# Duo attention and an MLP on one core: the program's order written anew, a zero fill in two copies

## The chip, the cores and the metric

The kernel runs on one core of one Trainium2 chip. Its time is the device time of one execution in microseconds, the median of several runs. A profiled execution gives the trace, whose span runs from the first to the last instruction.

## The reference, cut

```python
# q, k, v: 4 batches x 8 heads x 768 positions x 64, float32
keep[retrieval heads 0, 2, 6] = causal
keep[other heads]             = causal & (key is one of the first 4 | query - key < 64)
a = softmax(where(keep, q @ k.T / 8, -1e9));  x = (a @ v) as 3072 tokens x 512
h = x @ w_in                                  # 512 -> 2048
g = maximum(h, 0) + alpha * minimum(h, 0)     # alpha: one slope for each of the 2048
out = g @ w_out                               # 2048 -> 512, float32
```

## The kernel before

The 32 heads are 16 pairs, numbered n = 0 to 15, four to a batch: in a pair one head stands on partitions 0 to 63 and the other on 64 to 127. The 3072 tokens are eight pieces of the MLP, t = 0 to 7, two to a batch (512 and 256 tokens). Batch 0's attention comes first; from then on the MLP of one batch lies between the attention of the next, so that TensorE has work all along.

Nothing in the program is scheduled by a planner. Each step is an *item* with a name, and `ORDER` is a string of some 1240 names kept in the program. Python walks through it once, and each engine runs what it is given in just that order. The item, not the engine, decides where an instruction runs. So an engine whose next instruction waits for data holds up all that stands behind it on this engine.

The names that matter here (n is the pair, h the head in it, m a part, t the piece of tokens, f a block of the 2048):

- `L` loads of q, k, v on SyncE's DMA queue (SP); `Cq`, `Ck`, `Cv` casts to bf16, by GpSimd (POOL), ScalarE (ACT) or VectorE (DVE) for the first pairs, as the lists CQ, CK, CV say. `Cv` on GpSimd has copies of the sink rows with it (line 342).
- `Tq`, `Tk` transposes of q and k on TensorE (lines 404, 406), `tq`, `tk` the copies from PSUM into `qT` and `kT` (411; 429, 435 to 437). From pair 8 on `Dq`, `Dk` are DMA transposes on SP's queue instead.
- `kz0` to `kz3`, `qz`, `qz0`: zero fills of the parts of `kT` and `qT` that no copy writes, one `kz` for each of the first pairs. `kz2` alone is a copy of a zero by ScalarE.
- `S` scores (TensorE, lines 456, 473, 505, 544), `s` their exponentials on ScalarE (512, 560, 566), `m` masks on VectorE (522, 571).
- `A` the product with v (TensorE, 595), `r`, `a` the division by the sums on VectorE (607, 614) into `xn`.
- `X`, `x` the transposition of `xn` into `xT`: on TensorE for pairs 0 to 3 and 15 (628), by a DMA transpose on SP's queue for pairs 4 to 14 (622).
- `P` the first product of the MLP (648), `p` the relu of -h on ScalarE (653), `g` the slopes on VectorE (660). `P0.f` is cut into three items, `P2`, `P4`, `P6` into two, and the first of the two needs only the first three of the batch's four head pairs that `PAIRS` orders; `xT` of a batch comes from four `X`.
- `O0.s.u` the second product of piece 0 (668), quarter u of the 2048; `o0.s` copies and stores it by GpSimd's queue (678). For the pieces from 1 on the second product is made of seven block products: `Z`, `Q`, `b`, `D` (711, 726, 744, 692).
- `wi..` and `wo0` to `wo3` the loads of the weights, in six and four DMAs on GpSimd's queue (827, 832, 836). Quarter u of `O0.s.u` reads what `wo`u loads.
- `warm0` to `warm8`: matmuls of zeros into a bank that nobody reads (822), of 32, 3, 14, 4, 4, 4, 4, 4 and 4 instructions. They keep TensorE busy.

```python
    for name in ORDER:
        if not beside_burst(name):
            emit_burst()
        I[name]()
```

`emit_burst` gives the saved 64-row score matmuls of both heads of a pair to TensorE in turn. PSUM has eight banks, which items take and give in the order of `ORDER`.

Of the kernel before, what the change touches and what calls it, by code (L numbers as in the profile page):

```python
# [19 lines left out]
S2.0.2 X0 s2.0.1 x0 wi6 Tq3 S2.0.0 warm6 tk3.1 s2.0.2 A1.0 tq3 wi7 r1.0 s2.0.0 A1.1 S2.1.0 wi5 S3.0.0 r1.1 a1.0 Lv3 A2.0  # L20
Cv3.0 Lq4 a1.1 wi4 X1 x1 s2.1.0 s3.0.0 S3.0.1 r2.0 S2.1.1 Cv3.1 s3.0.1 P0.3.0 s2.1.1 S3.1.0 A2.1 a2.0 Lk4 Cq4 S3.1.1
s3.1.0 r2.1 Ck4.0 a2.1 s3.1.1 P0.0.0 A3.0 A3.1 r3.0 a3.0 P0.1.0 r3.1 Tq4 X2 a3.1 P0.2.0 X3 Lq5 Lk6 x2 Lq6 P0.3.1 wi2 x3
Lk5 P0.1.1 wi3 tq4 Ck4.1 P0.2.1 near1 P1.0 P0.2.2 P0.1.2 p0.2 P0.0.1 P0.0.2 Tk4 p0.1 tk4.0 P0.3.2 p1.0 g0.1 p0.0 ro1
g1.0 P0.14 Cq5 near0 P1.14 tk4.1 g0.0 wo1 P0.15 p1.14 P0.13 p0.15 Tq5 g0.15 Lq7 P1.2 p0.13 P0.8 wo0 Lk7 g0.2 g1.14 p0.3
wo3 p0.8 nr g0.3 P0.9 Cq6 p0.9 P0.11 P0.10 g0.8 g0.9 P1.8 tq5 Ck5.1 Ck5.0 g0.13 p0.11 P1.10 p0.14 wo2 P0.4.0 Tq6 g0.11
P0.5.0 P0.5.1 Lv5 g0.14 p1.8 g1.8 p1.2 kfz1 P1.6 p0.10 Lv6 P0.4.1 P0.5.2 g1.2 p1.10 P0.4.2 tq6 g1.10 p1.6 g0.10 Tk5 P0.6
g1.6 near2 ns tk5.0 P0.12 p0.6 g0.6 p0.5 S4.1.0 p0.4 P0.7 s4.1.0 p0.12 P1.12 Ck6.1 S5.0.0 g0.4 Ck6.0 O0.1.0 g0.12 tk5.1
p1.12 Tk6 g0.5 g1.12 p0.7 D1.0 O0.0.0 P1.4 tk6.1 g0.7 tk6.0 s5.0.0 O0.0.1 S5.1.1 S5.0.2 p1.4 S6.1.1 m4.1.0 D1.1 g1.4
S5.1.0 S4.0.1 Lv4 Ck7.1 O0.1.1 O0.0.2 s6.1.1 Cq7 O0.1.2 D2.1 S4.0.0 Z1.0.1 S5.1.2 s5.0.2 S6.1.2 s5.1.0 S4.1.2 s5.1.1
S4.0.5 s4.0.1 S4.0.3 Ck7.0 s4.0.0 s5.1.2 D2.0 O0.0.3 m5.1.0 O0.1.3 Lq8 m4.0.0 m5.1.1 s4.0.3 Cv5 s4.1.2 S4.1.5 S4.1.1  # L30
m4.0.1 s4.0.5 S4.0.4 S4.0.2 s6.1.2 O0.2.0 m5.0.2 O0.2.1 m4.0.3 S6.1.0 Cv4 m5.1.2 s4.0.4 Tk7 m4.0.5 Z1.0.3 o0.0 s4.1.1
m5.0.0 m4.0.4 A5.1 r5.1 s4.1.5 Lk8 a5.1 s4.0.2 s6.1.0 Cv6 A4.0 Ck8 Lk9 tk7.1 Tq7 tk7.0 O0.2.2 r4.0 S6.0.2 S5.0.1 O0.2.3
m6.1.2 tq7 S6.0.0 o0.1 m4.1.5 Q1.0.1 a4.0 s6.0.2 m6.1.0 m6.1.1 S6.0.3 S4.1.4 S4.1.3 s6.0.0 S6.0.4 s5.0.1 S7.1.1 Cq8
O0.3.0 s6.0.3 s4.1.3 o0.2 Z1.0.2 Lv7 m5.0.1 m6.0.3 s6.0.4 A5.0 Ck9 Lq9 s4.1.4 r5.0 S6.0.5 S7.0.0 m4.1.3 s6.0.5 s7.0.0
O0.3.1 A6.1 S6.0.1 a5.0 Dk8.0 m4.1.1 S7.1.0 m6.0.4 b1.1.0 s6.0.1 m6.0.0 m4.1.4 s7.1.1 O0.3.2 Cq9 S7.0.2 m6.0.5 Dq8
S7.0.1 A4.1 r6.1 Cv7 Dk9.0 a6.1 m7.1.1 O0.3.3 m6.0.1 s7.1.0 s7.0.1 r4.1 S8.1.1 s7.0.2 m7.0.2 S7.1.2 a4.1 S8.0.0 m7.0.1
S8.0.4 m7.0.0 s7.1.2 X5 o0.3 A6.0 s8.0.0 m7.1.0 A7.0 m7.1.2 s8.1.1 Dq9 r6.0 a6.0 A7.1 r7.0 Q1.0.2 S8.1.0 Lq10 S8.0.1
S9.0.0 s8.0.4 S9.0.1 S9.1.0 kfz2 r7.1 X4 X6 a7.1 a7.0 s8.0.1 s9.1.0 X7 nz0 Q1.0.5 D4.0 S8.0.5 Lk10 s9.0.1 Z1.0.4 S9.1.2
s9.0.0 m10.0.2 S9.0.2 Q1.0.6 b4.1.0 s8.1.0 Q1.0.3 S8.0.2 D3.0 S8.1.4 s8.0.5 b2.1.0 s9.1.2 S9.1.1 b7.1.0 S8.0.3 Lk11
s9.0.2 s8.0.2 Cq10 s8.1.4 P2.11.0 D4.1 P2.8.0 P2.3.0 b3.1.0 Lv9 s8.0.3 P2.4.0 P2.12.0 m8.0.1 m8.0.0 m9.0.2 P2.4.1  # L40
P2.12.1 m4.1.2 m9.0.0 Dq10 m9.1.2 s9.1.1 D3.1 p2.4 m8.1.0 P2.3.1 P2.8.1 m9.0.1 p2.3 m8.0.4 P2.2.0 m9.1.1 Q1.0.7 m9.1.0
b8.1.0 p2.12 m8.1.1 P2.7.0 P2.2.1 g2.4 P2.11.1 P2.7.1 p2.8 g2.3 p2.2 P2.1.0 g2.12 P2.6.0 P2.0.0 Lq11 P2.0.1 P2.1.1
P2.6.1 g2.8 m8.0.5 m8.0.3 Ck11 Lv8 p2.11 g2.2 P3.4 P2.5.0 p2.6 g2.11 Cv9 b5.1.0 Ck10 P2.13.0 p2.1 g2.6 p2.0 P2.5.1
P2.13.1 g2.1 p2.7 P2.10.0 P2.10.1 p2.5 g2.7 P3.12 Lv11 g2.5 p3.4 Dk11.0 A9.1 p2.10 g2.0 Q1.0.4 P2.14.0 p2.13 g2.10 p3.12
P2.9.0 r9.1 Cq11 P2.14.1 g3.4 P2.9.1 p2.9 Cv8 g2.13 b6.1.0 P2.15.0 g2.9 P2.15.1 Q2.1.1 p2.14 g3.12 P3.0 g2.14 Q2.0.1
b1.2.1 p2.15 a9.1 Lv10 g2.15 A8.0 r8.0 Q2.1.2 Dk10.0 S8.1.5 S8.1.3 b1.2.0 p3.0 Z2.1.1 S10.0.0 S10.0.5 a8.0 Z2.1.3 s8.1.5
Q2.0.2 Dk10.1 s10.0.0 Dq11 A9.0 s8.1.3 Lq12 Q2.1.5 b7.2.1 b7.2.0 S10.1.1 g3.0 s10.0.5 S10.0.1 b4.2.1 S11.0.0 S10.0.4
S11.1.1 S11.1.0 r9.0 Z2.1.2 a9.0 s11.0.0 s10.1.1 s11.1.1 Z2.0.1 m4.0.2 Q2.1.6 s11.1.0 s10.0.4 Z2.1.4 P3.8 S11.0.2
S11.0.1 S10.1.2 b2.2.1 m8.1.3 Lk13 Z2.0.3 b3.2.1 S10.1.0 Lv14 Q2.1.7 m11.1.0 Cv10 m10.1.1 Q2.1.3 Lq13 s10.0.1 S10.0.2
# [35 lines left out]
def kernel(  # L85
# [237 lines left out]
    def item(name, fn, *args):  # L323
        I[name] = lambda: fn(*args)
# [681 lines left out]
```

## Time and profile before

| | |
|---|---|
| median of 3 runs | 221.5 us (221.34 to 221.97) |
| the profiled execution's own time | 222.12 us |
| its span | 220.4 us, so 1.7 us lie around it |
| TensorE matmuls busy | 213.7 us, 97% |
| VectorE busy | 186.6 us, 85% |
| ScalarE busy | 146.4 us, 66% |
| GpSimd busy | 46.7 us, 21% |
| moved by DMA | 35.98 MB |

The profiled execution took 0.6 us more than the median of the runs. Busy time of TensorE is counted from pipelined matmuls, so a share of 97% says that it was hardly ever without an instruction, not that each column took its shortest time. Where TensorE waited is read from the start times in the timeline, and what it waited for from the releaser in brackets at the end of a row.

### The profile page before, as it was taken

The numbers are of one execution on the slowest core, as the hardware profiler recorded it, in microseconds if no ns is written. First come the engines' busy times: TensorE is split into PE (matmuls) and PEld (weight loads), VectorE is DVE, ScalarE is ACT, GpSimd is POOL, SyncE is SP. The second block draws the span as 40 slices with busy tenths as digits, with TensorE's granted clock in tenths as the row PEclk, the third lists the DMA queues.
The fourth block names the chain that finished last, engine by engine and source line by source line (L and its number), as shares of the span: only waits on it lengthen the run. The fifth ranks groups of instructions, "written<-read, shape, count | busy, mean of one in ns | idle before, by whom it ended". The sixth has DMA issues, their size and how long they took to land.

```text
span 220.4 us, 5765 instructions
## 1 busy us (share of the span) xinstructions
PE 213.7 (97%) x2194; PEld 158.0 (72%) x2210; DVE 186.6 (85%) x471; ACT 146.4 (66%) x314; POOL 46.7 (21%) x92
## 2 busy tenths in 40 slices
PE   8999999999999999999999999999999999999993
PEld 8788976665466765568789646678888645788882
DVE  6679658999989987999999999999999669799741
ACT  4689638999999794565972375589995066563330
POOL 6659990620412200003020200010010100000000
PEclk9999999999999999999999999999999999999999
DMA  5999999999999999999998699692027110011033
GB/s 170 329 212 212 313 240 226 233 204 210 205 241 199 224 179 230 222 186 192 205 232 157 147 244 201 143 206 70 4 97 111 51 48 0 3 48 48 3 145 142
DMA packets 89655, 35.98 MB, mean 163 GB/s; under 512 B 76676, under 2 KB 87964, under 8 KB 89628
## 3 DMA queue, kind: packets, MB, share of 16 engines
q1 hardware_dynamic: 83484, 26.35, 59.7%
q0 software_dynamic: 5824, 8.93, 17.7%
q8 instruction: 17, 0.28, 0.6%
q10 hardware_dynamic: 320, 0.34, 0.5%
q14 instruction: 10, 0.08, 0.1%
HBM read 27.58 MB, written 6.29 MB: 154 GB/s over the span
## 4 chain that ended last, share of the span: by engine, by line
PE 85%; DMA 7%; SPq 2%; POOL 2%; DVE 1%; issue 1%; ACT 0%; POOLq 0%
PE P L648 38%; PE P L726 27%; PE P L595 6%; PE P L668 6%; DMA rows<-in_k_dram 4%; PE P L473 4%; DMA xT<-xn 3%; PE P L406 2%; SPq L254 1%; PE P L466 1%; POOL w_in_b L827 1%; SPq L277 1%; PE P L628 1%; PE P L456 1%; DVE eS L571 1%
## 5 line engine op out<-in xcount | busy, mean ns | idle before, releaser
L648 PE MATMUL P<-xT,w_in_b 128*128 128x256 bf16 (+1 forms) x501 | 88.2, 325 | 1.0 <-DMA xT<-xn 0.4
L660 DVE SCALAR_TENSOR_TENSOR g<-neg,oma,P 128x256 bf16<-128x256 f32 (+1 forms) x128 | 72.0, 608 | 11.1 <-ACT neg L653 10.4
L653 ACT ACTIVATE neg<-P 128x512 f32<-128x512 f32 x96 | 55.1, 601 | 30.9 <-PE P L648 23.5
L648 PEld LDWEIGHTS <-w_in_b 128*128 128x128 bf16 x512 | 49.2, 98 | 30.3 <-DMA xT<-xn 0.7
L726 PEld LDWEIGHTS <-g 128*128 128x128 bf16 x480 | 45.6, 98 | 8.2 <-issue 1.0
L726 PE MATMUL P<-w_out_b,g 128*128 128x256 bf16 x320 | 40.0, 273 | 0.0
L512 ACT ACTIVATE eR<-P 128x448 bf16<-128x448 f32 (+4 forms) x63 | 36.6, 630 | 5.1 <-PE P L473 2.6
L744 POOL DMA_DIRECT2D out_dram<-ot x14 | 7.9, 565 | 113.9 <-ACT ot L768 46.7
L560 ACT ACTIVATE eS<-P 128x352 bf16<-128x352 f32 x45 | 20.1, 488 | 1.5 <-PE P L473 1.3
L614 DVE TENSOR_TENSOR xn<-P,rcp 128x448 bf16<-128x448 f32 (+1 forms) x32 | 18.7, 598 | 0.6 <-DVE rcp L607 0.2
L668 PE MATMUL P<-w_out_b,g 128*128 128x512 bf16 x59 | 15.1, 380 | 0.3
L571 DVE TENSOR_TENSOR eS<-eS,ms_near 128x352 bf16<-128x352 bf16 x45 | 14.7, 347 | 0.0
L711 DVE TENSOR_TENSOR g<-g 128x1024 bf16<-128x1024 bf16 x20 | 13.5, 684 | 0.1
L456 PE MATMUL P<-qT,kT 128*128 128x192 bf16 (+14 forms) x68 | 11.1, 251 | 0.2 <-ACT eS L566 0.2
L473 PE MATMUL P<-qT,kT 64*128 64x176 bf16 (+8 forms) x175 | 11.3, 250 | 0.0
L595 PE MATMUL P<-vb,eS 128*128 128x65 bf16 x260 | 10.8, 193 | 0.0
L595 PEld LDWEIGHTS <-eS 128*128 128x128 bf16 x260 | 9.9, 97 | 1.2 <-issue 0.2
L522 DVE TENSOR_TENSOR eR<-eR,mr_near 128x128 bf16<-128x128 bf16 (+5 forms) x54 | 10.2, 221 | 0.2 <-ACT eR L512 0.2
L726 PE MATMUL P<-w,g 128*128 128x256 bf16 x80 | 10.2, 273 | 0.0
L595 PE MATMUL P<-vb,eR 128*128 128x65 bf16 x276 | 10.1, 193 | 0.0
L473 PEld LDWEIGHTS <-kT 64*128 64x128 bf16 x175 | 6.8, 94 | 4.4 <-issue 4.0
L607 DVE RECIPROCAL rcp<-P 128x7 f32<-128x7 f32 (+1 forms) x32 | 6.0, 194 | 4.7 <-PE P L595 3.1
(130 smaller groups left out, 269.3 us busy)
## 6 DMA issues: line engine op xcount, KB each, us to landing
out_dram<-ot POOLq DMA_DIRECT2D x18, 256.0 KB, 3.2
rows<-in_k_dram SPq DMA_DIRECT2D x21, 192.0 KB
rows<-in_q_dram SPq DMA_DIRECT2D x18, 192.0 KB
rows<-in_v_dram SPq DMA_DIRECT2D x17, 192.0 KB
rows<-in_v_dram SPq DMA_DIRECT2D x14, 196.0 KB
rows<-in_q_dram SPq DMA_DIRECT2D x7, 384.0 KB
w_out_b<-in_moe_w_out_dram POOLq DMA_DIRECT2D x4, 512.0 KB, 16.2
rows<-in_k_dram SPq DMA_DIRECT2D x9, 196.0 KB
```

The lines of the kernel that those rows point to most:

```text
L473: nc.tensor.matmul(to, keys[own], queries[own], start=True, stop=True)
L512: nc.scalar.activation(ebuf[n, hh][:, lo:hi].rearrange("p (x c) -> p x c", x=len(parts)), P[:, got[0]:got[0] + len(parts), 0:(hi - lo) // ...
L560: nc.scalar.activation(slots, sc[:, 0:352].rearrange("p (s c) -> p s c", c=176), AF.Exp, scale=scale)
L571: nc.vector.tensor_tensor(slots, slots, ms_near[:, 0:2, :] if m == 0 else ms_near[:, 1:3, :], op=ALU.mult)
L595: nc.tensor.matmul(pav[:, i, :], e[:, o:o + 128], vv[:, j, hh, 0:D + 1], start=(m == 0), stop=(m == len(terms) - 1))
L614: nc.vector.tensor_tensor(xn[n][:, 0:nt, D * hh:D * hh + D], pav[:, :, 0:D], rcp.to_broadcast([128, nt, D]), op=ALU.mult)
L648: nc.tensor.matmul(psg[:, w * i:w * (i + 1)], w_in_b[:, c, 128 * fb:128 * (fb + 1)], xT[:, c, o:o + w], start=(x == 0), stop=(x == 3))
L653: nc.scalar.activation(neg[t, f], bank(held["P", t, f][0]), AF.Relu, scale=-1.0)
L660: nc.vector.scalar_tensor_tensor(g_buf[t % 2][:, fb, 0:w], neg[t, f][:, c], oma[:, fb:fb + 1], bank(got[0])[:, c], op0=ALU.mult, op1=ALU.add)
L668: nc.tensor.matmul(bank(held["O", t, s][0]), g_buf[t % 2][:, f, 128 * s:128 * (s + 1)], w_out_b[:, f, :], start=(f == 0), stop=(f == 15))
L711: nc.vector.tensor_tensor(to, x0, x1, op=op)
L726: nc.tensor.matmul(q_bank(t, u, CHAIN[y]), left[t, u][y][:, f, :], right[y][:, f, :], start=(first and f == 0), stop=(f == 7), skip_group_ ...
```

## The change

Two things differ. The zero fill of pair 2's half of `kT` becomes two copies, one for each head, `kz2` and `kz4`, so that they can stand at two places of the order:

```diff
-    item("kz2", nc.scalar.copy, kT_all[:, 2].rearrange("p h c -> p (h c)"), zero.to_broadcast([128, 2 * 7 * 128]))
+    for hh in range(2):
+        item(f"kz{2 * hh + 2}", nc.scalar.copy, kT_all[:, 2, hh], zero.to_broadcast([128, 7 * 128]))
```

And `ORDER` is written anew: nearly all of its lines differ. All other items are the same, and each stands once. SP's queue gets its loads and transposes in the same order as before. The lines of the program behind the fill move down by one. The first lines of the table:

```diff
-busy zero id warm0 kz3 Lq0.0 sz1 vz2 nms nmr so1 vz0 Lq0.1 Lk1 warm8 warm5 warm3 kz1 qz0 one Lq1 Lk0 La Ck0.0 kz2 Cq0.0
-Tq0.0 tq0.0 Tk0.0 qz warm2 Lk2 Lq2 kz0 tk0.0 Ck1.0 Ck1.1 Cq0.1 Tk1 S0.0.1 s0.0.1 Tq0.1 S0.0.0 Cq1 warm7 Lv0 tk1.0 sz2
...
+busy zero id warm0 kz3 Lq0.0 sz1 vz2 nms nmr so1 vz0 Lq0.1 Lk1 Lq1 Lk0 La Cq0.1 Ck0.0 kz0 sz2 kz1 Cq0.0 idf qz0 Ck1.0
+warm8 Tq0.0 Ck1.1 kz4 Tk0.0 Lk2 tk0.0 warm2 tq0.0 Cq1 vo S0.0.0 kz2 Tk1 s0.0.0 S0.0.2 s0.0.2 kfz0 warm5 ro0 Ck0.1 vz1
...
```

Ahead of the first transposes TensorE had 44 matmuls of zeros (`warm0` with 32, `warm8`, `warm5` and `warm3` with 4 each); now it has 36 (`warm0`, `warm8`), and `warm5` and `warm3` come among the first scores. The sum over the program is the same.

ScalarE's first rows, from the cast of pair 0's keys on; before:

```order
L364 CAST g_85<-rows 128x6x64
L324 COPY kT<-zero 128x1792
L411 COPY qT<-P 64x768
L512 ACTIVATE eR<-P 128x896 x2
L411 COPY qT<-P 128x768
L512 ACTIVATE eR<-P 128x896
L566 ACTIVATE eS<-P 128x4x192
L512 ACTIVATE eR<-P 128x896
```

And with the change:

```order
L364 CAST g_85<-rows 128x6x64
L324 COPY kT<-zero 128x896
L411 COPY qT<-P 64x768
L324 COPY kT<-zero 128x896
L512 ACTIVATE eR<-P 128x896 x2
L411 COPY qT<-P 128x768
L512 ACTIVATE eR<-P 128x896
L566 ACTIVATE eS<-P 128x4x192 x2
L512 ACTIVATE eR<-P 128x896 x3
```

The first `L411` is `tq0.0`, the second `tq1`; the `eR` rows are pair 0's exponentials and the `eS` rows pair 1's. Half of the zero copy moved behind `tq0.0`, and the two first exponentials of pair 1 now come one behind the other.

VectorE in the same part of the program. The row `qT 128x4x16` is `qz`, the two rows of line 429 are `tk0.0`, and each three of lines 435 to 437 are the copies of pair 1's keys for one head (`tk1.0`, `tk1.1`). Before, up to `tk1.1`:

```order
L324 MEMSET qT 128x4x16
L324 MEMSET kT 128x896
L429 COPY kT<-P 64x258
L429 COPY kT<-P 64x510
L435 COPY kT<-P 64x6x124
L436 COPY kT<-P 64x20
L437 COPY kT<-P 64x7x4
L324 MEMSET eS 128x6x32
L324 MEMSET rows 128x128 x2
L435 COPY kT<-P 64x6x124
L436 COPY kT<-P 64x20
L437 COPY kT<-P 64x7x4
```

And with the change, from `tk0.0` to `qz`:

```order
L429 COPY kT<-P 64x258
L429 COPY kT<-P 64x510
L324 MEMSET vb 128x70
L324 MEMSET eR 128x164
L324 MEMSET rows 128x128
L435 COPY kT<-P 64x6x124
L436 COPY kT<-P 64x20
L437 COPY kT<-P 64x7x4
L435 COPY kT<-P 64x6x124
L436 COPY kT<-P 64x20
L437 COPY kT<-P 64x7x4
L324 MEMSET qT 128x4x16
```

`qz` stood ahead of `tk0.0`; now it stands behind both heads of `tk1`, ahead of `tq0.1`.

GpSimd among the first loads of weights; `g_85` are the casts of the first pairs' queries and keys, `vb` values. Before, from `wi1a`, `wi0a`, `wi1b`, `wi0b` (line 827) on:

```order
L827 DMA w_in_b<-in_moe_w_in_dram 64x2x512 x4
L351 CAST g_85<-rows 128x2x6x64
L391 CAST vb<-rows 128x14x64
L342 COPY vb<-vb 4x6x32 x2
L391 CAST vb<-rows 128x14x64
L342 COPY vb<-vb 4x6x32
L832 DMA w_in_b<-in_moe_w_in_dram 64x4x512 x3
```

And with the change:

```order
L827 DMA w_in_b<-in_moe_w_in_dram 64x2x512 x2
L391 CAST vb<-rows 128x14x64
L342 COPY vb<-vb 4x6x32 x2
L351 CAST g_85<-rows 128x2x6x64
L827 DMA w_in_b<-in_moe_w_in_dram 64x2x512 x2
L391 CAST vb<-rows 128x14x64
L342 COPY vb<-vb 4x6x32
L832 DMA w_in_b<-in_moe_w_in_dram 64x4x512 x2
```

Pair 1's values (`Cv1`) and pair 3's queries (`Cq3`) come between the first and the second half of the early weight loads instead of behind them. Further down the last two loads of `w_out_b` (`wo3`, `wo2`) now both stand behind the masks `nr` and `ns` (lines 794 to 812), where `wo3` stood ahead of both and `wo2` between them.

Further on: TensorE comes to the first matmul that reads `wo2` through `O0.1.2`, where it came to it through `O0.0.2`, and the scores `S4.1.0`, `S5.0.0`, `S6.1.1` that stood ahead of it stand behind it. GpSimd stores `o0.1`, `o0.2`, `o0.0`, `o0.3` in this order instead of 0, 1, 2, 3. The first product of piece 2 begins with `P2.7.0` instead of `P2.11.0`, after the same matmuls. Behind these the order within the pieces differs everywhere, with the same items.

More of the change, by code (lines that the diff above doesn't have):

```diff
@@ L20 @@
[L20 to L49, printed above, removed]
@@ L80 @@
-Q6.0.4 Z6.1.4 b3.7.0 b6.6.0 Z7.0.4 Q6.1.4 Q6.1.3 Q7.0.7 b7.6.1 b6.6.1 b8.6.1 b5.7.0 Q7.0.3 Q7.0.4 b8.7.0 b6.7.0
+busy zero id warm0 kz3 Lq0.0 sz1 vz2 nms nmr so1 vz0 Lq0.1 Lk1 Lq1 Lk0 La Cq0.1 Ck0.0 kz0 sz2 kz1 Cq0.0 idf qz0 Ck1.0
+warm8 Tq0.0 Ck1.1 kz4 Tk0.0 Lk2 tk0.0 warm2 tq0.0 Cq1 vo S0.0.0 kz2 Tk1 s0.0.0 S0.0.2 s0.0.2 kfz0 warm5 ro0 Ck0.1 vz1
+tk1.0 S0.0.1 tk1.1 qz Ck2.1 Al Tq1 Lq2 Tq0.1 Ck2.0 Lv0 Cq2 Lk3 warm4 warm3 tq0.1 tq1 Tk0.1 s0.0.1 sz0 S1.1.0 Cv0 s1.1.0
+Lv1 warm7 S1.0.0 Ck3.0 Ck3.1 tk0.1 Tk2 s1.0.0 Lq3 wi1a S0.1.0 warm6 so0 tk2.0 one wi0a s0.1.0 S0.1.1 Tq2 S0.1.2 Cv1 Cq3
@@ new lines @@
+s0.1.1 wi1b wi0b vz3 A0.0 S1.0.1 s0.1.2 al tk2.1 Lv2 A0.1 tq2 r0.0 S1.1.1 s1.0.1 r0.1 Tk3 S2.0.1 s1.1.1 a0.0 S2.0.2 a0.1
+A1.0 s2.0.1 tk3.0 r1.0 A1.1 Cv2 Lv3 a1.0 Lq4 r1.1 s2.0.2 Lk4 Tq3 S2.0.0 a1.1 Lq5 tq3 S2.1.0 X0 wi6 s2.0.0 X1 x1 s2.1.0
+wi7 Cv3.0 S3.0.0 x0 S2.1.1 A2.0 tk3.1 wi5 s3.0.0 wi4 S3.0.1 s2.1.1 so2 A2.1 Lk6 s3.0.1 Ck4.1 r2.0 Ck4.0 S3.1.0 a2.0
+P0.3.0 S3.1.1 wi2 s3.1.0 A3.0 s3.1.1 r2.1 a2.1 Cq4 Cv3.1 r3.0 P0.1.0 A3.1 a3.0 r3.1 P0.2.0 wi3 X2 P0.0.0 wo1 a3.1 X3 x2
+Cq5 Tk4 x3 tk4.1 tk4.0 P0.3.1 P1.2 P0.0.1 P0.1.1 P0.2.1 P0.1.2 wo0 P0.3.2 Tq4 p1.2 p0.1 P1.0 nr P0.0.2 Lq6 Tq5 p0.3 g1.2
@@ new lines @@
+s6.0.3 m5.0.1 s4.1.4 Ck9 O0.3.0 Cv6 Cv7 s4.1.0 s6.0.5 A5.0 A6.1 r5.0 s6.0.0 O0.3.1 r6.1 S7.1.1 a5.0 S7.1.0 S6.0.1 s4.1.3
+a6.1 S7.0.2 Lq9 m6.0.3 s7.1.1 Cq9 S7.0.0 S6.0.4 O0.3.2 m4.1.0 s6.0.1 O0.3.3 m4.1.4 s7.1.0 m4.1.1 m7.1.1 S7.0.1 m4.1.3
+Dk8.0 m7.1.0 s6.0.4 m6.0.5 m6.0.1 s7.0.2 s7.0.0 s7.0.1 m7.0.2 b1.1.0 Dq8 A4.1 Dk9.0 m6.0.4 S8.0.0 m7.0.0 r4.1 m6.0.0
+a4.1 S7.1.2 S8.0.4 m7.0.1 S8.1.1 s7.1.2 o0.3 A6.0 A7.0 m7.1.2 A7.1 Q1.0.2 r6.0 a6.0 r7.0 S8.0.1 s8.1.1 S8.1.0 s8.0.0
+S8.0.3 s8.0.4 X5 Q1.0.5 Dq9 r7.1 s8.0.1 S9.0.1 a7.1 s8.0.3 S9.0.0 S9.1.0 a7.0 m8.0.1 Z1.0.2 S9.1.2 S8.0.5 m8.1.1 s8.1.0
```

85 lines of the change are left out of this document (52 added, 33 removed).

## The prediction

> **What bounds the kernel now.** I read the page's shares and slices first, then the table of stretches, the chain that ended last, the waits of TensorE, and the timeline at the places that the waits name.
>
> ```profile
> PE 213.7 (97%) x2194; PEld 158.0 (72%) x2210; DVE 186.6 (85%) x471; ACT 146.4 (66%) x314; POOL 46.7 (21%) x92
> PE   8999999999999999999999999999999999999993
> DMA  5999999999999999999998699692027110011033
> PE 85%; DMA 7%; SPq 2%; POOL 2%; DVE 1%; issue 1%; ACT 0%; POOLq 0%
> ```
>
> TensorE (PE) is at work in every slice and makes 85% of the chain that ended last. The DMA engines are as full through the first 21 slices, some 116 us. So little is to be won: the program's matmuls are the same before and after, and a new order can only remove TensorE's waits, or bring some. This is the table of stretches (columns: stretch, its length, then busy time of PE, weight loads, DVE, ACT, POOL, the granted clock, DMA share, GB/s):
>
> ```profile
> 66.00:88.00 22.00, 21.41 (x244) 14.15 (x245) 19.64 (x62) 17.51 (x44) 3.56 (x6) 1.00 1.22 207
> 88.00:110.00 22.00, 21.89 (x211) 15.25 (x211) 21.41 (x45) 15.34 (x34) 2.05 (x4) 1.00 1.13 203
> 110.00:132.00 22.00, 21.95 (x230) 16.06 (x230) 21.41 (x62) 11.33 (x27) 2.51 (x4) 1.00 0.91 194
> ```
>
> From 88 to 132 us PE is busy to within 0.16 of 44 us, and VectorE (DVE) for 42.8 of 44: nothing to win, and DVE has 0.6 us of slack in each 22. From 66 to 88 us PE lacks 0.59 us. TensorE's waits by releaser, and the rows where they fall:
>
> ```profile
> PE P L406 <- DVE kT L437: 0.5, 1, 0.5
> PE P L456 <- ACT eS L566: 0.2, 1, 0.2
> PEld L406 <- POOL g L351: 0.3, 1, 0.3
> 1.05 4.61 PEld L822 LDWEIGHTS <-busy 128*128 128x128 bf16 x44 [1.05 <-DVE zero L324]
> 6.95 0.78 PEld L822 LDWEIGHTS <-busy 128*128 128x128 bf16 x14
> 81.53 0.33 PEld L648 LDWEIGHTS <-w_in_b 128*128 128x128 bf16 x3 [0.68 <-DMA xT<-xn]
> 75.20 6.29 DMA xT<-xn
> ```
>
> Three kinds. In the first 20 us TensorE waits 0.5 for the copies of pair 1's keys, 0.2 for an exponential, 0.3 for `Cq3`: 1.0 in all. It starts cold: the 44 matmuls of zeros stand 4.61 / 44 = 105 ns apart, and the 14 of `warm2` at 6.95 us 0.78 / 14 = 56 ns. And at 81.5 us it waits 0.7 for pair 4's transposition (`X4`, issued at 75.20, landed 6.29 later at 81.49), the first need of piece 2. Together that is all that the order can bring: about 2 us of 220.
>
> **The front, up to 30 us.** Eight matmuls of zeros move from the cold part to a warm one. Done cold they took 8 x 105 = 0.84 us, done warm 8 x 56 = 0.45: 0.39 gained, since pair 0's transposes fill the cold time instead. That they can start 0.8 us earlier rests on their casts:
>
> ```profile
> 3.91 0.68 DVE L355 CAST g<-rows 128x384 bf16<-128x384 f32 x1 [0.76 <-DMA rows<-in_q_dram]
> 4.10 0.51 ACT L364 CAST g<-rows 128x384 bf16<-128x384 f32 x1 [1.10 <-DMA rows<-in_k_dram]
> 4.52 1.68 ACT L324 COPY kT<-zero 128x1792 bf16<-128x1792 bf16 x1
> 10.36 0.79 ACT L411 COPY qT<-P 128x768 bf16<-128x768 bf16 x1
> 8.72 1.75 ACT L512 ACTIVATE eR<-P 128x896 bf16<-128x896 f32 x2 [1.20 <-PE P L505]
> ```
>
> They are done at 4.6, and 36 zeros end at 1.05 + 36 x 0.105 = 4.8. ScalarE's zero copy of 1.68 ends at 6.20; with the transposes earlier, `tq0.0` would come at some 5.9 and find ScalarE still busy. That is what the two copies are for: half of it (0.84) ends at 5.4, `tq0.0` runs at its data, and the other half fits into the 1.20 us in which ScalarE waits ahead of the first exponential. So the split costs nothing; the first exponential at 8.72 comes about 0.6 earlier.
>
> Against that stands a new wait. `tq1` on ScalarE writes into `qT`, which `qz` fills, and `qz` now stands behind both `tk1` on DVE:
>
> ```profile
> 9.91 0.94 DVE L435 COPY kT<-P 64x744 bf16<-64x744 bf16 x1
> 10.86 0.18 DVE L437 COPY kT<-P 64x28 bf16<-64x28 bf16 x1
> 4.55 0.11 DVE L324 MEMSET qT<- 128x64 f32 x1
> 11.43 0.25 PE L456 MATMUL P<-qT,kT 128*128 128x192 bf16 x1
> ```
>
> The second `tk1` ended at 11.04; without the fills between the two and with pair 1's transposes earlier I put it at 10.7. Then `qz` (0.11) and `tq1` (0.79) end at 11.6, where pair 1's first scores stood at 11.43. Behind `tq1` on ScalarE wait `s0.0.1` and pair 1's exponentials. Of the 0.6 gained the sum keeps little there, but TensorE has by then done more of pair 0's scores and zeros.
>
> `Cq3` (0.88) moves behind `Cv1` and ahead of two weight issues:
>
> ```profile
> 16.24 2.55 POOL L827 DMA_DIRECT2D w_in_b<-in_moe_w_in_dram  x4
> 18.75 0.88 POOL L351 CAST g<-rows 128x768 bf16<-128x768 f32 x1
> 19.51 0.98 POOL L391 CAST vb<-rows 128x896 bf16<-128x896 f32 x1
> 20.55 0.63 POOL L342 COPY vb<-vb 4x192 f32<-4x192 f32 x2
> 20.91 0.92 PE P L595 x26
> w_in_b<-in_moe_w_in_dram POOLq DMA_DIRECT2D x4, 128.0 KB, 6.3
> 30.09 2.38 PE P L648 x15
> ```
>
> Four issues of 0.64 stood ahead of it; now two and `Cv1` with its sinks (1.6): 2 x 0.64 - 1.6 = 0.3 later. But pair 1's product with v (`A1.0`, `A1.1`: 26 or 27 matmuls each, 0.92 in the row) now stands ahead of `Tq3` and covers that. The two issues that now come later (`wi1b`, `wi0b`) lose 1.6 for `Cv1` and 0.9 for `Cq3`, 2.5 in all; issued by 18.8 and 6.3 to landing they were there at some 25, and the first matmuls that need them (the chain's piece at 30.09) come 5 us behind that.
>
> The sum of the front lies between -0.3 (the wait for `qz` costs its 0.4, and nothing but 0.1 is saved) and 0.39 + 1.0 = 1.4. I take 0.5: the 0.39 and a little of the waits, being nearer to the row that is certain.
>
> **The middle, 49 to 56 us.** The front's gain meets a load:
>
> ```profile
> 41.17 0.76 POOL L836 DMA_DIRECT2D w_out_b<-in_moe_w_out_dram  x1
> DMA to landing us min/median/max: 13.6/16.2/20.2
> 54.30 2.76 PE L668 MATMUL P<-w_out_b,g 128*128 128x512 bf16 x12
> 51.16 0.86 PE P L668 x4
> ```
>
> `wo2`, issued last at 41.17, lands not before 41.17 + 13.6 = 54.8. Its first reader before is the fifth of the twelve matmuls at 54.30, so at 54.30 + 4 x 2.76 / 12 = 55.2: 0.4 of room. In the new order three items of scores no longer stand ahead of the first reader; their five matmuls have 448 + 4 x 176 = 1152 columns, and 4 x 512 took 0.86 us, so they are 0.5 us. With the front's 0.5 TensorE stands there at 55.2 - 0.5 - 0.5 = 54.2 and waits 0.6, so that the gain is gone and 0.1 with it. An earlier issue would not help: the other three, issued by 31.9, are ahead of it in the same queue. So I cost this at -0.6 of the front's +0.5, with bounds of 0 (it lands 0.6 earlier) and -1.0 (0.4 later).
>
> **80 us.** Whatever is left is held at `X4`. The SP queue has the same order; landing 81.49 was late because loads and GpSimd's store of `o0.3` lie beside it:
>
> ```profile
> 75.53 0.54 POOL L678 DMA_DIRECT2D out_dram<-ot  x1 [5.93 <-ACT ot L674]
> 61.45 0.58 POOL L678 DMA_DIRECT2D out_dram<-ot  x1 [1.60 <-ACT ot L674]
> 75.20 4.86 SPq L622 DMA_TRANSPOSE xT<-xn  x3
> ```
>
> TensorE reaches piece 2 after the same matmuls, before at 81.53 - 0.68 = 80.85, now 0.1 later, and the wait shrinks to 0.6. The landing alone decides the time: what it comes earlier, up to 0.6, is won in full, what it comes later is lost in full. The profile shows no reason for either, so I take the same landing, with bounds of -0.6 and +1.5 (two transposes delayed, below).
>
> **Behind 82 us** the order changes and TensorE had no wait. DVE's 0.6 us of slack in 22 us is the cover; I cost it at 0, at worst 0.5.
>
> **Sum.** Front -0.5, middle +0.6: 0.1 late at `X4`, whose wait of 0.7 takes that in; behind it 0. So on the profiled execution 222.12 + 0 = 222.1 (a span of 220.4 and 1.7 around it). The profiled execution took 0.6 more than the median of the runs; the forecast on the scale of the runs is 222.1 - 0.6 = **221.5**.
>
> **Rivals.**
> *Faster: the loads are no anchors.* `wo2` lands 0.6 earlier, since fewer of SP's packets lie beside it, and `X4` too, since its neighbours are ordered anew. For it: both landings were taken in a queue full of other traffic. Against: bytes and SP's order are the same. With the front's gain of 0.5, or 1.0 where more of its waits go, and 0.4 to 0.7 at `X4`, that is 0.9 to 1.7: 219.8 to 220.6. If only one of both happens it is at most 0.6, 220.9, which belongs to the forecast.
> *Slower: the store of `o0.0` falls among the transposes.* It was issued at 61.45 and now follows `o0.1` and `o0.2`, which were issued at 66.21 and 69.05. The rows that show it:
>
> ```profile
> 69.05 0.54 POOL L678 DMA_DIRECT2D out_dram<-ot  x1 [1.96 <-ACT ot L674]
> 68.82 1.99 SPq L381 DMA_TRANSPOSE kT<-natk  x1
> 71.33 1.23 SPq L622 DMA_TRANSPOSE xT<-xn  x1
> ```
>
> A transpose issued beside a store held the SP queue for 1.99, one without for 1.23. If the store delays `Dk9.0`, `X5` and `Dq9` by 0.76 each, up to two of them ahead of `X4`, `X4` lands 0.8 to 1.5 later: 222.3 to 223.0. It decides from a landing later than 81.5 + 0.7.
> *Hidden loss: the cold part lasts longer.* The step from 105 to 56 ns came after 5.5 us of nearly unbroken work. If transposes do not count for it, the new front has 36 instead of 44 matmuls ahead, and the step would come some 3 us later; half of 3 us is 1.5, less the front's 0.5 a delay of 1.0, of which the waits of the front (up to 0.7 in the rows of keys and exponentials) and `X4`'s 0.7 hide all or all but 0.3: 221.5 to 221.8. So it decides only if `X4` lands earlier. The Trainium skill, "TensorE: Matmul & The Clock Gate", says in "Part 4: PE-mode transpose" that a transpose does not count as activity in the same way, and in "Part 1: The HAM clock gate" that the windows are free-running, so that the step may fall otherwise from run to run. By that rule the time would be the 221.8 at most of this rival; no row here shows a cold part with fewer matmuls.
> *Slower: masks late on DVE.* From 88 us on the new order makes an `A` wait for a mask: 0.3 to 0.7, 221.8 to 222.2.
>
> **Chances.** Forecast (221.5, its own range 220.9 to 222.1) 0.40; loads no anchors 0.31; stores 0.17; masks 0.07; cold part 0.05. A measurement of this kernel tells about 0.3%, 0.7 us, from no change: 220.8 to 222.2. Faster by more than that is the first rival, 0.31; slower the stores, the masks at their upper end (0.04) and losses of the new order that I can't name (0.08, taken from the forecast), 0.29; within it the rest, 0.40. The range leaves out the first rival's best third and the stores' worst cases: 220.3 to 222.9.
>
> **What would show it.** Right: the first exponential near 8.1; `tq1` waiting for DVE; the first products of piece 0 at 30 us 0.3 to 0.7 earlier; a wait of TensorE of about 0.5 at line 668 for `w_out_b`, and at 81 us one for `xT`. Wrong: no wait at 668, a landing of `X4` outside 80.8 to 82, a second cold stretch of matmuls 107 ns apart behind 6.5 us, or waits behind 88 us.

## The result, and the profile after

| | median | executions | ratio to before, 95% interval |
|---|---|---|---|
| before | 221.56 us (220.79 to 222.14) | 14 | |
| changed | 222.47 us (221.75 to 228.08) | 14 | 1.0041 (1.0023 to 1.0059) |
| changed, a second time | 223.02 us (222.01 to 225.9) | 12 | 1.0071 (1.0048 to 1.0093) |
| changed, a third time | 222.27 us (221.65 to 223.97) | 12 | 1.0048 (1.0026 to 1.0070) |

The change is a loss of 0.8 to 1.6 us, 0.4 to 0.7%, each round against executions of the kernel before beside it (medians 221.56, 221.43 and 221.49). Ratios, here and below, leave out single executions more than 1.5% above the fastest of their kernel (228.08 and 225.9 here, 226.09, 225.69 and 249.12 below), so they differ a little from quotients of the medians. The changed kernel scatters more: 6.3, 3.9 and 2.3 us between its lowest and highest execution in the three rounds, where before had 1.4, 1.6 and 1.8. (In the two other groups of runs before itself scattered by 2.7 and 2.4.) Forecast was 221.5 and no difference; the time lies in the range, but the loss was not forecast. The execution that was profiled with the first result took 228.08 and is told of below only where its extremes help; the profile that follows is the second time's, 223.33 us at a span of 221.6.

TensorE's waits, with their engine, line and releaser, in that profile:

```profile
PE P L822 <- DVE zero L324: 1.1, 1, 1.1
PE P L473 <- ACT eS L560: 0.7, 1, 0.7
PE P L595 <- DVE vb L342: 0.6, 1, 0.6
PE P L456 <- ACT qT L411: 0.4, 1, 0.4
```

The three waits that the front had before are gone, and so is the wait for `X4`. In their place stand three others: 0.4 for `tq1`, 0.6 for a copy of sink rows, 0.7 for an exponential. The stretches by engine (columns as in the prediction):

```profile
22.00:33.00 11.00, 10.40 (x155) 8.35 (x153) 8.22 (x20) 6.28 (x11) 9.55 (x18) 1.00 1.17 254
55.00:66.00 11.00, 10.18 (x103) 5.75 (x101) 9.69 (x31) 9.14 (x26) 3.22 (x3) 1.00 1.16 209
66.00:77.00 11.00, 10.91 (x169) 7.26 (x166) 9.42 (x36) 10.16 (x25) 2.72 (x5) 1.00 0.94 163
77.00:88.00 11.00, 11.00 (x94) 6.60 (x91) 10.46 (x29) 8.76 (x24) 1.14 (x3) 1.00 1.20 221
88.00:110.00 22.00, 22.00 (x212) 15.34 (x210) 21.62 (x47) 14.90 (x32) 1.86 (x3) 1.00 1.23 215
110.00:132.00 22.00, 22.00 (x240) 16.45 (x235) 21.19 (x59) 12.11 (x28) 3.26 (x4) 1.00 0.93 201
```

The same two stretches before:

```profile
22.00:33.00 11.00, 10.89 (x162) 8.95 (x163) 6.51 (x19) 5.63 (x11) 10.69 (x18) 1.00 1.15 276
55.00:66.00 11.00, 10.89 (x108) 6.15 (x109) 10.01 (x31) 10.69 (x29) 2.89 (x3) 1.00 1.12 222
```

From 66 us on TensorE lacks next to nothing. In this execution it loses in two stretches: from 22 to 33 us, where it lacks 0.60 (the copy of sink rows), and from 55 to 66, where it lacks 0.82; before, it lacked 0.11 in each. The experiments tell which of the two moves the median. This is the timeline of the second, of TensorE, ScalarE and VectorE:

```profile
56.85 1.90 PE L668 MATMUL P<-w_out_b,g 128*128 128x512 bf16 x8
58.68 0.51 PE L473 MATMUL P<-qT,kT 64*128 64x176 bf16 x6
59.88 0.37 PE L473 MATMUL P<-qT,kT 64*128 64x176 bf16 x5 [0.69 <-ACT eS L560]
...
57.82 0.56 ACT L512 ACTIVATE eR<-P 128x448 bf16<-128x448 f32 x1
59.37 0.46 ACT L560 ACTIVATE eS<-P 128x352 bf16<-128x352 f32 x1 [0.98 <-DVE eS L817]
...
57.68 0.33 DVE L571 TENSOR_TENSOR eS<-eS,ms_near 128x352 bf16<-128x352 bf16 x1
57.94 1.28 DVE L692 TENSOR_TENSOR g<-w_out_b,g 128x1024 bf16<-128x1024 bf16 x2
59.17 0.10 DVE L816 MEMSET eS<- 128x48 f32 x1
59.23 0.09 DVE L817 MEMSET eS<- 128x32 f32 x1
```

Read it from below. `near1`, two fills of 0.1 us that turn the second buffer of exponentials to the layout of the later pairs, stands on VectorE behind `D2.1` and `D2.0` (line 692, 1.28 us). The exponential that writes this buffer waits 0.98 us for them on ScalarE, and so TensorE waits 0.7 for a PSUM bank. Before, `near1` stood among the first products of piece 0, behind `P0.2.1`, and ran 28.5 us earlier:

```profile
30.64 0.10 DVE L816 MEMSET eS<- 128x48 f32 x1
```

The beginning of piece 2, the first matmul of line 648 behind 80 us, was at 81.53 us before and is at 82.54 here. From there to the span's end are 138.9 us before and 139.1 here.

### The profile page after: what moved, and what is told of

The parts are those of the page before. It is cut to its first block, busy times and chain, and to the rows that moved or that the text cites. A ratio compares the mean times of both kernels' runs of the same rounds, so it can differ in the third digit from the quotient of the medians.

```text
span 226.3 us, 5783 instructions
## 1 busy us (share of the span) xinstructions
PE 216.0 (95%) x2194; PEld 159.3 (70%) x2210; DVE 189.6 (84%) x471; ACT 146.8 (65%) x315; POOL 47.5 (21%) x92
## 4 chain that ended last, share of the span: by engine, by line
PE 81%; DVE 8%; DMA 6%; issue 2%; ACT 2%; DVEq 0%; ACTq 0%
PE P L648 36%; PE P L726 26%; PE P L595 6%; DMA qT<-natq 3%; DMA xT<-xn 3%; PE P L473 3%; PE P L822 2%; PE P L406 2%; PE P L456 2%; PE P L668 2%; DVE g L660 1%; PE P L628 1%; DVE vb L342 1%; DVE natk L364 1%; DVE kT L435 1%
## 5 line engine op out<-in xcount | busy, mean ns | idle before, releaser
L648 PEld LDWEIGHTS <-w_in_b 128*128 128x128 bf16 x512 | 49.7, 99 | 30.4 <-issue 0.5
L726 PE MATMUL P<-w_out_b,g 128*128 128x256 bf16 x320 | 39.5, 273 | 0.1
L512 ACT ACTIVATE eR<-P 128x448 bf16<-128x448 f32 (+4 forms) x63 | 36.0, 622 | 5.2 <-PE P L473 3.1
L744 POOL DMA_DIRECT2D out_dram<-ot x14 | 8.7, 624 | 112.3 <-ACT ot L768 37.1
L571 DVE TENSOR_TENSOR eS<-eS,ms_near 128x352 bf16<-128x352 bf16 x45 | 14.1, 330 | 0.7 <-ACT eS L560 0.6
L473 PE MATMUL P<-qT,kT 64*128 64x176 bf16 (+10 forms) x174 | 11.6, 251 | 1.9 <-DVE g L660 0.9
L522 DVE TENSOR_TENSOR eR<-eR,mr_near 128x128 bf16<-128x128 bf16 (+5 forms) x54 | 10.7, 222 | 1.8 <-ACT eR L512 1.7
L456 PE MATMUL P<-qT,kT 128*128 128x192 bf16 (+13 forms) x68 | 11.3, 250 | 0.4 <-ACT qT L411 0.4
```

The costliest lines, as they stand in the source:

```text
L456: nc.tensor.matmul(to, keys, queries, start=True, stop=stop)
L473: nc.tensor.matmul(to, keys[own], queries[own], start=True, stop=True)
L512: nc.scalar.activation(ebuf[n, hh][:, lo:hi].rearrange("p (x c) -> p x c", x=len(parts)), P[:, got[0]:got[0] + len(parts), 0:(hi - lo) // ...
L571: nc.vector.tensor_tensor(slots, slots, ms_near[:, 0:2, :] if m == 0 else ms_near[:, 1:3, :], op=ALU.mult)
L648: nc.tensor.matmul(psg[:, w * i:w * (i + 1)], w_in_b[:, c, 128 * fb:128 * (fb + 1)], xT[:, c, o:o + w], start=(x == 0), stop=(x == 3))
L726: nc.tensor.matmul(q_bank(t, u, CHAIN[y]), left[t, u][y][:, f, :], right[y][:, f, :], start=(first and f == 0), stop=(f == 7), skip_group_ ...
```

## The experiments

Three theories stood against each other: the front with the copy of line 342 (1), the part between 55 and 90 us (2, later A for the fills alone), and the order behind 82 us. The first four runs cut the two orders at some 30 us and put them together crosswise; `order of before` and `order of the change` are the two tables, and an item stands at the first place that it gets. (Where the order of before is used, its one zero copy is the two copies, one behind the other.)

**The changed kernel again.**

> The changed kernel once more, for a profile of a typical execution beside the one of 228 us. Theory 1 (VectorE's cast and sink copy of pair 3's values meets GpSimd's casts and weight issues; the copy of line 342 took 2.00 us there and 0.38 before): in a typical execution the same copy is longer than 0.38 but shorter than 2.0, and TensorE waits 0.3 to 1 us for it ahead of pair 3's second product with v. Theory 2 (transposes and stores between 60 and 90 us): the copy is at 0.4, and the loss of 0.9 us shows as waits of TensorE between 55 and 90 us. 222.3 to 222.6 by both.

223.02 us, above what either theory gave. The copy took 1.13 and the wait was 0.6, as theory 1 has it, and the wait of 0.7 at 60 us is theory 2's. Which of them makes the end late the next three ask.

**The changed order to 30 us, then that of before.**

```diff
-... x2 Cq5 Tk4 x3 tk4.1 tk4.0 P0.3.1 P1.2 P0.0.1 P0.1.1 P0.2.1 ...
+... x2 Cq5 Tk4 x3 tk4.1 tk4.0 Tq4 Lq6 P0.3.1 Lk5 P0.1.1 tq4 P0.2.1 near1 ...
```

> The changed order up to the first product that needs the third pair of piece 0 (some 30 us), the order of before behind it. Theory 1: it keeps the copy among GpSimd's issues, so 222.2 to 222.6, slower than before by 0.6 to 1.0. Theory 2: the loss is behind 30 us, so 221.0 to 221.6.

221.55 us, ratio 1.0010 (0.9990 to 1.0030): no loss that can be told from nothing, so theory 1 falls. (A late front could hide in the wait for `X4`; the run with `X4` first, below, has no such wait and is level too.) Its profile has the front's gain and where it is lost:

```profile
81.11 4.95 PE L648 MATMUL P<-xT,w_in_b 128*128 128x512 bf16 x22 [0.46 <-DMA xT<-xn]
74.89 6.17 DMA xT<-xn
```

TensorE was 0.4 earlier there than before and waited for `X4`, as the prediction has it for what the front gains. But `X4` landed 0.4 earlier as well, at 74.89 + 6.17 = 81.06, where the prediction took the same landing (81.49).

**The order of before to 30 us, then the changed one.**

```diff
-... P0.2.0 X3 Lq5 Lk6 x2 Lq6 P0.3.1 wi2 x3 Lk5 ...
+... P0.2.0 X3 Lq5 Lk6 x2 Lq6 Ck4.1 wi2 wi3 wo1 Cq5 Tk4 x3 tk4.1 tk4.0 P0.3.1 ...
```

> The order of before up to some 30 us, the changed order behind it. Theory 1: 221.2 to 221.8, as before. Theory 2: 222.2 to 222.8.

223.01 us in six executions, ratio 1.0076 (1.0051 to 1.0100): the whole loss, and more. It has the wait at line 473, and one of 0.45 for another exponential at the beginning of piece 2:

```profile
59.43 0.37 PE L473 MATMUL P<-qT,kT 64*128 64x176 bf16 x5 [0.89 <-ACT eS L560]
82.45 6.16 PE L648 MATMUL P<-xT,w_in_b 128*128 128x512 bf16 x27 [0.45 <-ACT eR L512]
```

**The cast and the sink copy of pair 3's second values earlier.**

```diff
-... Cq4 Cv3.1 r3.0 ...
+... x0 S2.1.1 A2.0 tk3.1 Cv3.1 wi5 ...
```

> The changed kernel with one thing else: VectorE's cast of pair 3's second values with its sink copy stands ahead of the divisions of pair 2 (behind the copies of pair 3's keys) instead of behind them. Theory 1: the copy takes 0.4 us and the wait ahead of pair 3's second product with v goes; 221.3 to 221.8, and no execution above 223. Theory 2: 222.3 to 222.6, unchanged.

223.28 us, ratio 1.0084 (1.0055 to 1.0112). A miss: theory 1 gave 221.3 to 221.8, theory 2 no more than 222.6. It says less than it was made for. The copy took 0.25 us, but the cast now stood ahead of `so2`, the fill of the third buffer of exponentials, and TensorE waited for that fill instead:

```profile
24.49 0.23 PE L595 MATMUL P<-vb,eS 128*128 128x65 bf16 x2 [0.60 <-DVE eS L324]
```

One wait of 0.6 took the place of another, and the wait at 59 us stayed. So this run does not refute theory 1; the two before speak against it as the cause of the loss.

The next four test the fills alone and the part behind 81 us.

**The fills early.**

```diff
-... Lv4 near0 p1.14 ... D2.0 O0.0.3 near1 m5.1.1 ...
+... Lv4 near0 near1 p1.14 ... D2.0 O0.0.3 m5.1.1 ...
```

> The changed kernel with one thing else: the two small fills that turn the second of the three buffers of exponentials to its later layout (lines 816, 817) stand on VectorE right behind the first buffer's, at some 46 us, instead of behind the sums of w_out quarters at 59 us. Theory A (ScalarE waits 1.0 us for them, and TensorE 0.7 to 1.1 for the exponentials behind): that wait goes; what stays is the wait for the sink copy at 27 us and the landing of pair 4's transposition, which hides part of the gain: 221.9 to 222.4, 0.4 to 0.9 less than the changed kernel. Theory B (the loss is spread over the transposes, and VectorE's fills only stand beside it): 222.6 to 223.1, unchanged.

222.11 us, ratio 1.0020 (0.9990 to 1.0050), where the three rounds of the changed kernel had 1.0041 to 1.0071: in theory A's range, though the interval takes in the lowest of the three. The wait at 60 us is gone, and piece 2 begins at 81.73.

**The fills early and the cast early.** Both of the diffs above in one.

> Both moves in one: the fills early, and VectorE's cast and sink copy of pair 3's second values ahead of pair 2's divisions. Theory A: both waits of the changed order are gone and the front's gain of 0.5 is held at pair 4's transposition: 221.0 to 221.7. Theory B: 222.6 or more.

222.75 us, ratio 1.0050 (1.0029 to 1.0072), a miss; it is still below the run with the cast alone (1.0084), from which it differs by the fills only. The wait that the cast's place makes was there in the run before, and is here again, 0.77 us; the expectation left it out:

```profile
25.64 0.23 PE L595 MATMUL P<-vb,eS 128*128 128x65 bf16 x2 [0.77 <-DVE eS L324]
```

**The kernel before with the fills late.**

```diff
-... tq4 Ck4.1 P0.2.1 near1 P1.0 ...
+... D2.0 near1 O0.0.3 ...
```

> The kernel before (with its zero fill as two copies, one behind the other) and one move: the same fills late, behind the last of the sums of w_out quarters. Theory A: TensorE waits some 1 us near 58 us, of which the wait of 0.6 for pair 4's transposition takes in 0.6: 221.7 to 222.3. Theory B: 221.3 to 221.6.

222.23 us, ratio 1.0016 (0.9992 to 1.0041): the median lies in A's range, but the interval takes in no change, and the wait that A expects is not there. The fills ran late, but nobody waited:

```profile
58.52 0.10 DVE L816 MEMSET eS<- 128x48 f32 x1
58.59 1.44 ACT L512 ACTIVATE eR<-P 128x448 bf16<-128x448 f32 x3
59.86 0.52 ACT L560 ACTIVATE eS<-P 128x352 bf16<-128x352 f32 x1
```

In the old order the exponentials of the next 1.4 us go to another buffer (`eR`), and the next into `eS` comes at 59.86. So it is not the late place alone that costs, but the place together with the order of the scores. In the changed order undoing it pays, in this group and in the next.

**The order of before to 81 us, then the changed one.**

```diff
-... S8.0.3 Lk11 s9.0.2 s8.0.2 Cq10 s8.1.4 P2.11.0 D4.1 P2.8.0 ...
+... S8.0.3 Lk11 s9.0.2 s8.0.2 Cq10 s8.1.4 m4.1.2 m6.0.2 s8.0.3 m8.0.1 m8.1.1 D4.1 m8.1.0 m8.0.2 P2.7.0 ...
```

> The order of before up to the first product of piece 2 (81 us), the changed order behind it. Theory A: the late part costs nothing, 221.2 to 221.7. Theory B, and the case of late masks: 222 or more.

221.38 us, ratio 1.0004 (0.9980 to 1.0028). The late part costs nothing that can be told, and the masks on VectorE that the prediction gave a chance make no wait.

The third group asked for what stays beside the fills, and tried the anchor at `X4`.

**The order of before to 30 us, then the changed one, the fills early.** Two of the diffs above in one.

> The order of before up to 30 us, the changed order behind it, as in the run that gave 223.0, and the fills of the second exponentials' buffer early (46 us). Theory A (the fills' place is the loss): 221.5 to 222.2, 0.8 to 1.5 less than without the move. Theory B: 222.7 to 223.3.

222.35 us, ratio 1.0035 (1.0015 to 1.0055), where it was 1.0076 without the move: less, as A has it, but 0.15 above its range. Its profile has a new wait:

```profile
74.25 0.56 PE L473 MATMUL P<-qT,kT 64*128 64x448 bf16 x8 [1.02 <-DMA qT<-natq]
...
67.14 2.44 SPq L358 DMA_TRANSPOSE qT<-natq  x1
67.14 6.97 DMA qT<-natq
...
65.62 0.57 POOL L678 DMA_DIRECT2D out_dram<-ot  x1 [4.94 <-ACT ot L674]
66.58 1.43 POOL L678 DMA_DIRECT2D out_dram<-ot  x1 [0.39 <-ACT ot L674]
68.14 0.54 POOL L678 DMA_DIRECT2D out_dram<-ot  x1
```

`Dq8`, the transposition of pair 8's queries, stands between the stores of `o0.2` and `o0.0`, held SP's queue for 2.44 us, and landed at 74.1, 7 us behind its issue. Whether the stores are the reason the profiles leave open: with the store of `o0.0` at its old place `Dq8` held the queue for 2.05, 2.13 and 2.28 us in three of them, and with the three stores in a row for only 1.22 in the run with the fills early alone, where TensorE did not wait for it.

**The fills early, the sink copy on ScalarE.**

```diff
-        sinks(n, vv.rearrange("p t h c -> p h t c"), [hh], (nc.gpsimd.tensor_copy, nc.vector.tensor_copy)[hh])
+        sinks(n, vv.rearrange("p t h c -> p h t c"), [hh], (nc.gpsimd.tensor_copy, nc.scalar.copy)[hh])
-... s3.1.0 A3.0 s3.1.1 r2.1 a2.1 Cq4 Cv3.1 r3.0 ...
+... s3.1.0 A3.0 Cv3.1 s3.1.1 r2.1 a2.1 Cq4 r3.0 ...
```

> The changed kernel with the fills early, and the copy of pair 3's sink rows on ScalarE instead of VectorE, between two exponentials, with VectorE's cast ahead of the second division of pair 2. If the copy beside GpSimd's casts is what is left of the loss and of the spread: 221.2 to 221.9, no execution above 222.8, and no wait at 27 us. If not: 222.1 as with the early fills alone, with the same spread up to 223.

222.26 us (221.44 to 223.38), ratio 1.0029 (1.0009 to 1.0048): a miss. The wait at 27 us is gone and the scatter is as it was. In its profile the front lost 1.4 us to another wait, for the keys of pair 1, whose load came late; the profile of the fills early alone has the same wait, at 0.5:

```profile
7.88 0.51 POOL L364 CAST g<-rows 128x384 bf16<-128x384 f32 x1 [2.17 <-DMA rows<-in_k_dram]
8.44 0.51 PE L406 MATMUL P<-ident,g 128*128 128x128 bf16 x6 [1.41 <-POOL g L364]
```

**The kernel before, `X4` ahead of pair 10's loads.**

```diff
-... Q1.0.2 S8.1.0 Lq10 S8.0.1 ... X4 X6 a7.1 ...
+... Q1.0.2 S8.1.0 X4 Lq10 S8.0.1 ... X6 a7.1 ...
```

> The kernel before with one move: pair 4's transposition stands on SP's queue ahead of the loads of pair 10's queries, not behind. The prediction's reading, that its landing alone decides the time there: it lands about 1.0 earlier, the wait of 0.6 at 81 us goes, 220.8 to 221.0. Rival: with its neighbours as they are it lands no earlier, or another wait takes its place: 221.4 to 221.7.

221.50 us, ratio 0.9992 (0.9972 to 1.0012): the rival. The wait at 81 us is gone from its profile and piece 2 begins at 81.04, 0.5 earlier, but the median doesn't move by what can be told from nothing: 0.5 us would be 0.9977, inside the interval.

**The changed order to 30 us, then that of before, with `X4` first.** Two of the diffs above in one.

> The changed order up to 30 us, the order of before behind it, and pair 4's transposition ahead of the loads of pair 10's queries. If the front's gain of 0.5 was lost at that landing: 220.3 to 220.7, 0.9 to 1.2 less than the same kernel without the move (221.55). Rival: the front gains nothing that lasts, 220.9 to 221.2.

221.40 us, ratio 1.0009 (0.9983 to 1.0035). Piece 2 begins at 80.66 in its profile, 0.9 earlier than before, with a span of 219.3; its executions lie between 220.54 and 222.97, and the medians show no gain: above what either side expected. So I found no order that beats the kernel before.

The last three ask whether the store of `o0.0` makes `Dq8` late. The first two have the fills early and this diff, one with the front of before and one with the changed front; the third is the changed kernel beside them.

```diff
-... m5.0.2 o0.0 S6.0.5 ...
+... S6.1.2 Cv4 m6.0.2 s4.0.5 s5.0.1 s5.1.2 Z1.0.3 o0.0 Cq8 ...
```

> The order of before up to 30 us, the changed order behind it, the fills early, and the store of o0.0 (with ScalarE's copy) back at its old place, some 6 us ahead of the other two. Theory C (three stores in a row make the transposition of pair 8's queries late): the wait of 1.0 us at 73 us shrinks to 0.3 or less, 221.4 to 221.9. Theory D (the transposition is late for another reason, the buffer it writes or the loads): 222.2 to 222.6, as without the move.

> The changed kernel with the fills early and the store of o0.0 back at its old place. Theory C: 221.3 to 221.9, level with the kernel before. Theory D: 221.9 to 222.4.

> The changed kernel itself, on the same chip as the two others: 222.4 to 223.1 by both theories, 0.4 to 1.5 above the two.

222.05 us with the front of before, ratio 1.0027 (1.0009 to 1.0045), and 221.69 with the changed front, 1.0017 (0.9999 to 1.0035); the changed kernel beside them 222.27, 1.0048 (1.0026 to 1.0070), a little below what was expected of it. The second is in theory C's range, the first between C's and D's. In the profile of the first the wait for `Dq8` is gone, and the list of TensorE's waits has nothing behind 14 us:

```profile
PE P L822 <- DVE zero L324: 1.1, 1, 1.1
PE P L406 <- DVE kT L437: 0.5, 1, 0.5
PE P L456 <- ACT eS L566: 0.2, 1, 0.2
...
80.17 6.00 PE L648 MATMUL P<-xT,w_in_b 128*128 128x512 bf16 x27
```

That execution was the fastest of its kernel, 221.01, and its median is 1.0 above it. By the medians the store's place is worth 0.3 and 0.4 (222.35 to 222.05, 222.11 to 221.69, each pair measured on two chips), by the ratios less than 0.1%, well within the intervals: the store's part is not shown. Fills and store together are worth 0.6 on one chip, 222.27 to 221.69 with twelve executions each.

The move of the fills alone stands in three pairs of runs, each ratio against before in its own round: 1.0041 to 1.0071 and 1.0020 (changed kernel), 1.0076 and 1.0035 (front of before), 1.0084 and 1.0050 (cast early). All three fall, by 0.2 to 0.5%, and TensorE's wait at line 473 for the exponential of line 560 is in all five profiles with the changed order there and late fills (0.4 to 0.9 us) and in none of the six with early ones. But a part of the loss stays. Of the six kernels with early fills, four are slower than before by more than their intervals: 1.0027, 1.0029 and 1.0035, and 1.0050 with the wait that the early cast makes. What makes the 0.2 to 0.35% of the others is open.

The profiles of single executions agree on one thing: from the first matmul of piece 2 to the span's end it is 138.7 to 139.3 us in each of these, so in these executions what a kernel gains or loses is decided ahead of piece 2.

| | piece 2 begins, us | span, us |
|---|---|---|
| before | 81.53 | 220.4 |
| changed, second and third time | 82.54, 81.21 | 221.6, 220.3 |
| fills early | 81.73 | 221.0 |
| fills early, store at its old place | 80.47 | 219.5 |
| front of before, changed rest | 82.45 | 221.3 |
| the same, fills early; and store moved | 81.73, 80.17 | 220.4, 218.9 |
| changed front, rest of before | 81.11 | 219.9 |

## Why the prediction was right and wrong

**What bounds it: right; what can be won: read too high.** TensorE is at work in every slice, and the late part is neutral. Two of the waits that make up the 2 us are rows of weight loads (PEld), 0.3 for `Cq3` and 0.7 for `X4`. No matmul waited for `Cq3`, and the matmuls' own row at `X4` in the profile of before has 0.44:

```profile
81.53 4.99 PE L648 MATMUL P<-xT,w_in_b 128*128 128x512 bf16 x21 [0.44 <-DMA xT<-xn]
```

So the matmuls' waits were 0.5, 0.2 and 0.44, some 1.1 us, and no run here won a part of it that the medians can tell.

**The front: right in what it names, with one wait not seen.** In the first profile (228 us), pair 0's transposes began at 5.01 (5.86 before), the first exponential at 8.12 (8.72), as worked out. `tq1` waited for `qz`:

```profile
10.99 0.80 ACT L411 COPY qT<-P 128x768 bf16<-128x768 bf16 x1 [1.06 <-DVE qT L324]
11.84 0.24 PE L456 MATMUL P<-qT,kT 128*128 128x192 bf16 x1 [0.43 <-ACT qT L411]
```

That wait, 0.4 of TensorE, is the one that the prediction priced. The gain of 0.5 shows in the profile in which the front stands alone: with the rest of before piece 2 is reached 0.4 earlier; the median does not show it. Not seen was what the move of `Cv3.1` on VectorE, from 25 to between 25.8 and 26.5 us, puts beside GpSimd's next casts and weight issues. The rows of the second time, and then two of the profile at 228 us:

```profile
26.69 1.13 DVE L342 COPY vb<-vb 4x192 f32<-4x192 f32 x1
26.86 0.84 POOL L351 CAST natq<-rows 128x768 bf16<-128x768 f32 x1
27.87 0.49 PE L595 MATMUL P<-vb,eS 128*128 128x65 bf16 x11 [0.60 <-DVE vb L342]
```

```profile
27.43 2.00 DVE L342 COPY vb<-vb 4x192 f32<-4x192 f32 x1
29.48 0.49 PE L595 MATMUL P<-vb,eS 128*128 128x65 bf16 x11 [1.81 <-DVE vb L342]
```

A copy of 4 x 192 elements takes 0.25 us in seven other profiles; these two end 0.1 and 0.2 us after a cast of GpSimd has ended. The front's bound of -0.3 left that out. It makes single executions late; as the cause of the median's loss the runs speak against it, since the changed front with the rest of before is level with before, with the wait for `X4` and without.

**The middle at `wo2`: in one profile of three, at half the size.** The wait for `w_out_b` that the prediction put at line 668 is there in the third time's profile, in which the copy took 0.25 us, at 0.3 instead of 0.6:

```profile
54.34 1.02 PE L668 MATMUL P<-w_out_b,g 128*128 128x512 bf16 x4 [0.29 <-DMA w_out_b<-in_moe_w_out_dram]
58.72 0.37 PE L473 MATMUL P<-qT,kT 64*128 64x176 bf16 x5 [0.44 <-ACT eS L560]
```

In the other two, where the copy had cost 0.6 and 1.8, there is none, which the prediction named as a sign against it: TensorE keeps the front's gain up to there only in some executions.

**Between 56 and 80 us: the step that failed.** The prediction's sum has no term there. It went from `wo2` straight to `X4` ("TensorE reaches piece 2 after the same matmuls, before at 81.53 - 0.68 = 80.85, now 0.1 later") and looked for waits where TensorE waits for DMAs. It followed VectorE's order in the first 11 us and behind 88, not between. There the fills stood behind 1.28 us of sums, with an exponential behind them: a term of 0.4 to 0.9 for TensorE. Of the median it is 0.2 to 0.9 in the changed kernel (222.27 to 223.02, and 222.11 with the fills early) and 0.7 with the front of before (223.01 and 222.35), on different chips. The sum took these fills at nothing without a reason; what counts is not their 0.1 us but who is queued behind them. The fills are the largest part of the loss that the runs show; the 0.2 to 0.35% that stays without their wait has no cause shown, and lies by the crosswise runs in the order between 30 and 81 us too.

**`X4`: the wait is there, that it decides the time is not shown.** The changed front with the rest of before waits there; the changed kernel comes too late to wait. The prediction has what the landing comes earlier "won in full". With `X4` ahead of pair 10's loads piece 2 began 0.5 earlier in the profile, and the median was 221.50 beside 221.53 of before; a gain of 0.5 is neither shown nor excluded by the interval.

**The rival of the stores: the mechanism half right, the place wrong.** The store of `o0.0` falls among the transposes, but what TensorE then waits for is `Dq8` at 74 us (1.0), not `X4` at 81. That wait is 0.3 in the profile at 228 us and 1.0 in one of the four profiles with the fills early and the store late, absent from the other three. That the measured 222.47 lies in this rival's range is luck as far as the runs show: the wait that they show to cost most is the fills'.

**The cold part: not seen.** The 14 zeros of `warm2` stand 0.78 / 14 = 56 ns apart, as before, and begin 0.5 us earlier, so the delay of some 3 us that this rival took did not come:

```profile
6.43 0.78 PEld L822 LDWEIGHTS <-busy 128*128 128x128 bf16 x14 [0.17 <-issue]
```

## What to carry to other kernels

When an order is rewritten, walk every engine's queue between two anchors of the critical one: a fill of 0.1 us that moves behind 1.3 us of other work can be a wait of 1 us for what stands behind it on the next engine (in the changed order it was, in the old one nobody waited). A wait that is taken away at one place shows the next one behind it, here a load, a buffer's layout, a transposition and another transposition within 25 us, and a gain of 0.5 at the front reached no median here. In a kernel at 97% of its bound, the scatter of single executions (1.4 to 2.7 us for the kernel before) is larger than most steps, so profiles tell where, and only medians tell how much; a dozen executions each left intervals of 0.2 to 0.3% to each side.
